# Key weights in two loads, a different head of the program and a new written order, in a fused attention and gated-mixer block

## The chip, the cores and the metric

The kernel runs on one core of one Trainium2 chip. The metric is the device time of one execution in microseconds, from launch to end; the time of before is the median of three runs. Beside it there is one profiled execution, whose instruction span is a little shorter than its own time.

## The reference

For 2048 tokens of width 512 (16 tiles of 128 tokens), all in bf16:

```
h  = x + A(layernorm(x))          # linear attention, 32 heads of 16
h2 = h + B(layernorm(h))          # gated mixer, inner width 896
A:  q, k, v = x @ wqkv
    pq, pk = phi(q), phi(k)       # phi(t) = t + 1 if t > 0 else exp(t), plus 1e-6
    kv = sum_s pk * v ; z = sum_s pk
    out = (pq @ kv) / (pq @ z) @ wo
B:  z1, z2 = gelu(x @ w_in), halves of 896
    g = w_sp @ layernorm(z2) + b_sp        # w_sp is 2048 x 2048, over tokens
    out = (z1 * g) @ w_out
```

## The kernel before

The program is recorded first as a list of 804 operations, each with its engine and with what it reads and writes. Two lists written into the file decide the rest: `ORDER` gives the order in which the operations are put on their engines (each of the five engines then runs its own part of it strictly in that order, waiting on semaphores for what it reads), and `SLOT` gives each temporary tile its place in a pool, among others the bank of the accumulator memory. The costs and due times that stand beside the operations in the code no longer decide anything.

The input x is loaded by SP in eight transfers (tiles 0, 1, 2-3, and after the key weights 4-5, 6-7, 8-9, 10-11 and 12-15), all issued by line L492. The key weights, columns 512 to 1024 of wqkv, come as one load of 512 KB, called wk, after tiles 2-3; the query weights, wq, come last.

The head then works tile by tile. VectorE computes mean and variance (statistics L568, their combination L572). 1/sigma is made in one of two ways: for tiles 0 to 3, one at a time, by ScalarE as a logarithm and an exponential (L582, L584); for tiles 4 to 15, in pairs, by GpSimd as an addition and a power (L587, L589). VectorE normalises (L603). Tiles 0 to 5 are transposed by TensorE (L633, four products of 128 columns) and copied out by ScalarE (L640). Tiles 6 to 15 are transposed by DMA, issued by SP (L625). With the transposed tile as weights, four products of 512 columns over the four blocks of the contraction make a tile's keys (L715). Pairs of tiles share a two-bank accumulator and go through phi: an exponential (L692) and in half the cases a relu (L694) on ScalarE, then VectorE (L695, and L698 or L701). The products L747 accumulate normalised x against phi of the keys, and L729 makes the queries.

TensorE begins with idle products of a constant (L556), so that it runs while x is on its way: a chain of 8 of 512 columns (`WARM`), then 4 more of 512, and 4 of 256 columns between the first transposes, 16 in all.

After the sums over all tiles (sum of keys L759, its transpose L772, the value product L796, the product with wo L814), four groups of 512 tokens each get their denominators (L829), their logarithm and exponential on ScalarE (L834, L836), a spreading product (L844), the output projection (L879) and the second layernorm. Value weights wv, output weights wo and w_in are issued on GpSimd's queue behind the last DMA transpose, in the order wv, w_in, wo. Then come the products with w_in (L911 and L942), the token mixer (L981, 448 products of 512 columns) and the last projection (L999) with its addition on VectorE (L1005) and the stores from SP (L1007). The last token tile is projected and stored in two halves of 256 columns.

Of the kernel before, what the change touches and what calls it, by code (L numbers as in the profile page):

```python
# [5 lines left out]
FP32 = mybir.dt.float32  # L6
BF16 = mybir.dt.bfloat16
ACT = mybir.ActivationFunctionType
ALU = mybir.AluOpType

P = 128
# [1 line left out]


ORDER = [
# [36 lines left out]
]  # L52
SLOT = [
# [6 lines left out]
]  # L60


# [292 lines left out]
def bass_sequential_preLN__linear_attn_block__mixer_gmlp__prompt_kernel(  # L355
# [25 lines left out]
    K_RELU = (1, 3, 5, 7)  # L381
    CENTRED = ()
    A_STATS = ()
    R_POOL = (4, 6, 8, 10, 12, 14)
    COPY_DVE = ()
    LN1 = [[0], [1], [2], [3], [4, 5], [6, 7], [8, 9], [10, 11], [12, 13], [14, 15]]
    N2_ACT = range(16)
    VIA_ACT = ((0, 0), (1, 0), (2, 0), (3, 0))
# [83 lines left out]
    def bank(i):  # L472
        return lambda a: a[:, i, :]
# [17 lines left out]
    def load(eng, name, dst, src, nbytes, bias=0.0, behind=(), cost=0.5):  # L491
        o = op(eng, cost, lambda e: e.dma_start(dst.ap(), src), w=[dst], dma=(name, False), nbytes=nbytes,  # L492
               bias=bias, land=2.3)
        for p in behind:
            o.deps[p] = True
        return o
# [10 lines left out]
    load_x("sp", 0, 1)  # L507
    load_x("sp", 1, 2)
    load_x("sp", 2, 4)
    load("sp", "wk", wqkv[:, D:2 * D], w3[:, :, D:2 * D], D * D * 2 + 50000)  # L510
    for a in (4, 6):
        load_x("sp", a, a + 2)
    for a in (8, 10):
# [95 lines left out]
    def normalise_act(dst, src, rs, nm, n=512):  # L609
        op("act", act_c(n, 2) + 0.04, lambda e: e.activation(dst.ap(), src.ap(), ACT.Identity, bias=nm.ap(), scale=rs.ap()),  # L610
           r=[src, rs, nm], w=[dst])

    def minus(m, rs, nm):
        op("pool", 0.25, lambda e: e.tensor_scalar(nm.ap(), m.ap(), -1.0, None, op0=ALU.mult), r=[m], w=[nm])
        op("pool", 0.25, lambda e: e.tensor_tensor(nm.ap(), nm.ap(), rs.ap(), ALU.mult), r=[nm, rs], w=[nm])
# [31 lines left out]
    for grp in LN1:  # L647
# [21 lines left out]
        rs_op[grp[0]] = g.ops[-1]  # L669
        for i, n in enumerate(grp):  # L670
            d = xn1[n, :]
            normalise(d, x[n, :], Row(st_x, n), 6, rs[i:i + 1], negative=n in A_STATS)
            transposed(n, lambda d=d: d, xT, n in X_BY_PE)

    for gate, n, cost, count in ((first[0], 512, 2 * MM, 3), (rs_op[0], 512, 2 * MM, 1), (tr_op[0], 256, MM, 2),
                                 (tr_op[1], 256, MM / 2, 2)):
        for i in range(count):
            keep_busy(n, cost, [], [gate] if gate.eng != "pe" else [])
            if gate.eng == "pe":
                g.ops[-1].after.append(gate)  # L680
# [25 lines left out]
    def kv_proj(p, col):  # L706
        t = Tile(PS, 2)
        for ti in range(2):
            n = 2 * p + ti
            lhs = xcT[:, n * P:(n + 1) * P] if n in CENTRED else xT[n // TPG][:, (n % TPG) * P:(n % TPG + 1) * P]  # L710
            rhs = wqkv[:, col:col + D]

            def mm(e, ti=ti, lhs=lhs):
                for c in range(KD):
                    i = e.matmul(t(bank(ti)).ap(), lhsT=lhs.ap()[:, c, :], rhs=rhs.ap()[:, c, :], start=(c == 0),  # L715
                                 stop=(c == KD - 1))
                return i
            k_pe.append(op("pe", 4 * MM, mm, r=[lhs, rhs], w=[t()]))
        return t

    def q_proj(gq, f):
# [294 lines left out]
                for n in range((tg - 1) * TPG, tg * TPG):  # L1016
                    project(n, [(0, D)])
    for n in range((NG - 1) * TPG, NT):
        project(n, [(0, D)] if n < NT - 1 else [(0, D // 2), (D // 2, D)])


    g.schedule()
# [55 lines left out]
```

## Time and profile before

| | us |
|---|---|
| median of three runs (243.93 to 244.29) | 244.26 |
| the profiled execution's own time | 243.96 |
| its instruction span | 242.2 |
| TensorE busy in the span | 238.3 |
| VectorE, ScalarE, GpSimd busy | 135.2, 85.1, 34.1 |

The granted TensorE clock is listed as 1.000 over the span. The busy time of TensorE includes the idle products at the start. Matmuls overlap in the records, so how long a product holds the engine is read from the distance of the starts, not from the listed duration.

### The profile page before, as it was taken

Reading aid. Unit: us, or ns where it says so; the run is one execution under the profiler, and the core shown is the slowest. Engines: PE = TensorE matmul, PEld = TensorE weight load, DVE = VectorE, ACT = ScalarE, POOL = GpSimd, SP = SyncE. Lnnn points to the kernel's source line nnn. Section 1 sums busy time; section 2 is a strip of 40 time slices with the busy share of each in tenths; the row PEclk is TensorE's granted clock in tenths of the full one; section 3 lists DMA queues with packets and bytes.
Section 4 is the critical chain, followed back from the end, with each engine's and each line's share of the span. In section 5 each row is a group of like instructions: output and inputs, shape, how many; then the busy total and the mean of one; then the engine's idle time right before and its main releaser. Section 6 shows DMA issues by size and latency. Waiting matters only on the chain.

```text
span 242.2 us, 3026 instructions
## 1 busy us (share of the span) xinstructions
PE 238.3 (98%) x1175; PEld 108.8 (45%) x1175; DVE 135.2 (56%) x269; ACT 85.1 (35%) x107; POOL 34.1 (14%) x87
## 2 busy tenths in 40 slices
PE   8999999999999999999999999999999999999995
PEld 3544443433444444445444444444444444444443
DVE  4999654589999967656533223251332513322443
ACT  3875744898588598564500010000000000000000
POOL 5316021002316542122100000000000000000000
DMA  6920459954324231459344444446200100000022
GB/s 199 321 43 18 94 106 337 232 122 96 46 43 128 47 46 22 87 119 231 88 108 92 107 86 95 100 108 94 83 0 0 65 24 0 0 0 3 0 87 87
DMA packets 55598, 21.57 MB, mean 89 GB/s; under 512 B 49472, under 2 KB 54720, under 8 KB 55584
## 3 DMA queue, kind: packets, MB, share of 16 engines
q1 hardware_dynamic: 54640, 17.05, 32.7%
q0 software_dynamic: 944, 4.33, 5.5%
q8 instruction: 9, 0.15, 0.3%
q14 instruction: 5, 0.04, 0.1%
HBM read 7.47 MB, written 2.10 MB: 40 GB/s over the span
## 4 chain that ended last, share of the span: by engine, by line
PE 91%; DVE 4%; DMA 2%; ACT 2%; SPq 1%; issue 0%
PE ps L981 40%; PE ps L942 10%; PE ps L911 10%; PE ps L999 10%; PE ps L747 6%; PE ps L879 5%; PE ps L715 5%; PE ps L729 4%; DMA xh<-in_A_x_dram 2%; DVE small L568 1%; SPq L492 1%; DVE xT_pq_z L698 1%; DVE xh L884 0%; DVE xT_pq_z L859 0%; DVE e L695 0%; PE ps L844 0%
## 5 line engine op out<-in xcount | busy, mean ns | idle before, releaser
L981 PE MATMUL ps<-wsp,pk_xn_z 128*128 128x512 bf16 x336 | 73.8, 379 | 0.0
L988 DVE TENSOR_TENSOR e<-ps,e 128x512 bf16<-128x512 f32 x28 | 19.4, 691 | 66.0 <-PE ps L981 66.0
L981 PEld LDWEIGHTS ps<-wsp,pk_xn_z 128*128 128x128 bf16 x336 | 32.8, 98 | 39.5
L942 PE MATMUL ps<-hT,win 128*128 128x512 bf16 x112 | 26.6, 379 | 0.0
L911 PE MATMUL ps<-win,hT 128*128 128x512 bf16 (+1 forms) x128 | 26.0, 353 | 0.0
L999 PE MATMUL ps<-wout,xT_pq_z 128*128 128x512 bf16 (+1 forms) x119 | 24.7, 367 | 0.0
L981 PE MATMUL ps<-wqkv_wsp,pk_xn_z 128*128 128x512 bf16 x112 | 24.3, 379 | 0.0
L947 ACT ACTIVATE xT_pq_z<-ps 128x1024 bf16<-128x1024 f32 (+1 forms) x16 | 14.4, 913 | 23.9 <-PE ps L942 23.9
L568 DVE BATCH_NORM_STATS2 small<-xh 128x6 f32<-128x512 bf16 x32 | 20.7, 678 | 3.3 <-DMA xh<-in_A_x_dram 3.3
L920 DVE BATCH_NORM_STATS2 small<-pk_xn_z 128x6 f32<-128x512 bf16 (+1 forms) x32 | 18.3, 611 | 7.2 <-ACT pk_xn_z L916 7.1
L692 ACT ACTIVATE e<-ps 128x1024 bf16<-128x1024 f32 x16 | 16.5, 1029 | 9.7 <-PE ps L715 6.1
L911 PEld LDWEIGHTS ps<-win,hT 128*128 128x128 bf16 x128 | 12.5, 98 | 12.7 <-ACT e L854 0.3
L916 ACT ACTIVATE pk_xn_z<-ps 128x896 bf16<-128x896 f32 x16 | 14.5, 914 | 8.9 <-PE ps L911 8.8
L1005 DVE TENSOR_TENSOR e<-ps,xh 128x512 bf16<-128x512 f32 (+1 forms) x17 | 11.2, 660 | 11.3 <-PE ps L999 11.3
L999 PEld LDWEIGHTS ps<-wout,xT_pq_z 128*128 128x128 bf16 x119 | 11.6, 98 | 12.8
L981 PEld LDWEIGHTS ps<-wqkv_wsp,pk_xn_z 128*128 128x128 bf16 x112 | 11.0, 98 | 13.2
L942 PEld LDWEIGHTS ps<-hT,win 128*128 128x128 bf16 x112 | 10.9, 98 | 12.6 <-ACT pk_xn_z L916 0.4
L589 POOL TENSOR_TENSOR small<-small 128x2 f32<-128x2 f32 x22 | 16.0, 727 | 1.2
L587 POOL TENSOR_SCALAR small<-small 128x2 f32<-128x2 f32 x22 | 6.4, 297 | 67.6 <-DVE small L572 67.4
L747 PE MATMUL ps<-pk_xn_z 128*128 128x512 bf16 x64 | 15.6, 379 | 0.0
L729 PE MATMUL ps<-xT_pq_z,wqkv_wsp 128*128 128x512 bf16 x64 | 15.5, 380 | 0.0
L715 PE MATMUL ps<-wqkv_wsp,xT_pq_z 128*128 128x512 bf16 x64 | 15.3, 379 | 0.0
(72 smaller groups left out, 191.0 us busy)
## 6 DMA issues: line engine op xcount, KB each, us to landing
out_dram<-e SPq DMA_DIRECT2D x15, 128.0 KB, 1.7
win<-in_B_w_in_dram POOLq DMA_DIRECT2D x1, 1792.0 KB, 9.2
xh<-in_A_x_dram SPq DMA_DIRECT2D x5, 256.0 KB, 4.7
wqkv_wsp<-in_A_wqkv_dram SPq DMA_DIRECT2D x2, 512.0 KB, 5.7
wout<-in_B_w_out_dram POOLq DMA_DIRECT2D x1, 896.0 KB, 6.4
wsp<-in_B_w_sp_dram SPq DMA_TRANSPOSE x48, 2.9
xh<-in_A_x_dram SPq DMA_DIRECT2D x1, 512.0 KB, 6.2
wqkv_wsp<-in_A_wqkv_dram POOLq DMA_DIRECT2D x1, 512.0 KB, 4.8
```

Source lines behind the costliest of these rows:

```text
L568: op("dve", dve_c(512), lambda e: e.bn_stats(s6.ap(), src.ap()), r=[src], w=[s6])
L589: return op("pool", 0.7, lambda e: e.tensor_tensor(dst.ap(), dst.ap(), h.ap(), ALU.pow), r=[dst, h], w=[dst])
L692: op("act", act_c(n), lambda e: e.activation(lo.ap(), t(flat).ap(), ACT.Exp), r=[t()], w=[lo])
L715: i = e.matmul(t(bank(ti)).ap(), lhsT=lhs.ap()[:, c, :], rhs=rhs.ap()[:, c, :], start=(c == 0), stop=(c == KD - 1))
L729: r_ = e.matmul(t(bank(i)).ap(), lhsT=lhs.ap()[:, c, :], rhs=rhs.ap()[:, c, :], start=(c == 0), stop=(c == KD - 1))
L747: r = e.matmul(txk[h](bank(i)).ap(), lhsT=xx.ap()[:, c * P:(c + 1) * P], rhs=kk.ap(), start=(n == 0), stop=(n == NT - 1))
L911: k = e.matmul(t(bank(i)).ap()[:, 0:b - a], lhsT=l.ap()[:, c, :], rhs=win[c, a:b].ap(), start=(c == 0), stop=(c == KD - 1))
L920: op("dve", dve_c(b - a), lambda e, s6=s6, src=src: e.bn_stats(s6.ap(), src.ap()), r=[src], w=[s6])
L942: k = e.matmul(t(bank(i)).ap(), lhsT=l.ap()[:, c, :], rhs=r_.ap()[:, c, :], start=(c == 0), stop=(c == KD - 1))
L981: k = e.matmul(t(bank(0)).ap(), lhsT=l.ap()[:, s - a, :], rhs=r_.ap()[:, s - a, :], start=(s == 0), stop=(s == NT - 1))
L988: op("dve", dve_c(512), lambda e: e.tensor_tensor(gb().ap(), t(bank(0)).ap(), bsp().ap()[:, tg * GW:(tg + 1) * GW], ALU.add), r=[t(), bsp( ...
L999: k = e.matmul(t(bank(0)).ap()[:, 0:b - a], lhsT=l.ap()[:, fc, :], rhs=wout[fc, a:b].ap(), start=(fc == 0), stop=(fc == KF - 1))
```

## The change

There are five edits to the text of the program, and two new lists.

- The key weights are loaded in two transfers of 256 KB, wk0 with the first two contraction blocks and wk1 with the other two. SP issues one more DMA ahead of tiles 4 to 15.
- The key products of tiles 0 and 1 are two operations of two products each, so that the first two wait for wk0 alone.
- There are 3 gated idle products after the chain of 8 instead of 8: two of 512 columns and one of 256, 11 in all.
- `R_POOL` no longer has the pair of tiles 4 and 5: its 1/sigma is made by ScalarE.
- The last token tile is projected and stored as 384 and 128 columns.
- `ORDER` and `SLOT` are written anew for the 802 operations. Other options that the diff adds (`N1_POOL`, `N1_ACT`) are empty and make no instruction.

```diff
-    R_POOL = (4, 6, 8, 10, 12, 14)
+    R_POOL = (6, 8, 10, 12, 14)
+    K_SPLIT = (0, 1)
...
-    load("sp", "wk", wqkv[:, D:2 * D], w3[:, :, D:2 * D], D * D * 2 + 50000)
+    for i in range(2):
+        load("sp", f"wk{i}", wqkv[2 * i:2 * i + 2, D:2 * D], w3[:, 2 * i:2 * i + 2, D:2 * D], D * D + 25000)
...
-    for gate, n, cost, count in ((first[0], 512, 2 * MM, 3), (rs_op[0], 512, 2 * MM, 1), (tr_op[0], 256, MM, 2),
-                                 (tr_op[1], 256, MM / 2, 2)):
+    for gate, n, cost, count in ((first[0], 512, 2 * MM, 2), (tr_op[0], 256, MM, 1)):
...
-            rhs = wqkv[:, col:col + D]
-
-            def mm(e, ti=ti, lhs=lhs):
-                for c in range(KD):
-                    i = e.matmul(t(bank(ti)).ap(), lhsT=lhs.ap()[:, c, :], rhs=rhs.ap()[:, c, :], start=(c == 0),
-                                 stop=(c == KD - 1))
-                return i
-            k_pe.append(op("pe", 4 * MM, mm, r=[lhs, rhs], w=[t()]))
+
+            for c0, c1 in ((0, 2), (2, KD)) if n in K_SPLIT else ((0, KD),):
+                part_r = wqkv[c0:c1, col:col + D]
+
+                def mm(e, ti=ti, lhs=lhs, c0=c0, c1=c1, part_r=part_r):
+                    for c in range(c0, c1):
+                        i = e.matmul(t(bank(ti)).ap(), lhsT=lhs.ap()[:, c, :], rhs=part_r.ap()[:, c - c0, :],
+                                     start=(c == 0), stop=(c == KD - 1))
+                    return i
+                k_pe.append(op("pe", (c1 - c0) * MM, mm, r=[lhs, part_r], w=[t()]))
...
-        project(n, [(0, D)] if n < NT - 1 else [(0, D // 2), (D // 2, D)])
+        project(n, [(0, D)] if n < NT - 1 else [(0, D - P), (D - P, D)])
```

What the new lists do to the first instructions of each engine (numbers are tiles; tr is a transpose, K the key products, copy is L640):

```
TensorE before  12 idle, tr0, 2 idle, tr1, 2 idle, K0, tr2, K1, K2, tr3, tr4, tr5, K3, K4, queries ...
TensorE after   10 idle, tr0, 1 idle, tr1, tr2, K0, K1, tr3, K2, tr4, tr5, K3, K4, K5, ...
VectorE before  stat0 stat1 comb0 comb1 stat2 norm0 comb2 norm1 stat3 norm2 comb3 stat4 stat5 comb4 comb5
                norm3 stat6 stat7 norm4 norm5 ...
VectorE after   stat0 stat1 comb0 comb1 stat2 stat3 comb2 norm0 comb3 norm1 norm2 stat4 stat5 comb4 comb5
                norm3 stat6 norm4 norm5 ...
ScalarE before  1/s of 0, 1, 2, copy0 copy1, 1/s of 3, copy2, exp of keys 0-1, copy3 copy4 copy5 ...
ScalarE after   1/s of 0, 1, 2, ln of 3, copy0, exp of 3, copy1 copy2, 1/s of 4-5, exp of keys 0-1, copy3 copy4 copy5 ...
```

GpSimd's three weight loads come in the order w_in, wv, wo. The rest of the list reorders the same operations.

More of the change, by code (lines that the diff above doesn't have):

```diff
@@ L383, in bass_sequential_preLN__linear_attn_block__mixer_gmlp__prompt_kernel @@
     A_STATS = ()
-    R_POOL = (4, 6, 8, 10, 12, 14)
+    R_POOL = (6, 8, 10, 12, 14)
     COPY_DVE = ()
+    K_SPLIT = (0, 1)
+    N1_POOL = ()
+    N1_ACT = ()
     LN1 = [[0], [1], [2], [3], [4, 5], [6, 7], [8, 9], [10, 11], [12, 13], [14, 15]]
@@ L611, in normalise_act, with normalise_pool @@
            r=[src, rs, nm], w=[dst])
+    def normalise_pool(dst, src, m, rs):
+        op("pool", 0.9, lambda e: e.tensor_scalar(dst.ap(), src.ap(), m.ap(), rs.ap(), op0=ALU.subtract,
+                                                  op1=ALU.mult), r=[src, m, rs], w=[dst])
     def minus(m, rs, nm):
@@ L671, in bass_sequential_preLN__linear_attn_block__mixer_gmlp__prompt_kernel @@
             d = xn1[n, :]
-            normalise(d, x[n, :], Row(st_x, n), 6, rs[i:i + 1], negative=n in A_STATS)
+            if n in N1_POOL:
+                normalise_pool(d, x[n, :], st_x[n, 6:7], rs[i:i + 1])
+            elif n in N1_ACT:
+                nm = small([1], FP32)
+                minus(st_x[n, 6:7], rs[i:i + 1], nm.all())
+                normalise_act(d, x[n, :], rs[i:i + 1], nm.all())
+            else:
+                normalise(d, x[n, :], Row(st_x, n), 6, rs[i:i + 1], negative=n in A_STATS)
             transposed(n, lambda d=d: d, xT, n in X_BY_PE)
-    for gate, n, cost, count in ((first[0], 512, 2 * MM, 3), (rs_op[0], 512, 2 * MM, 1), (tr_op[0], 256, MM, 2),
-                                 (tr_op[1], 256, MM / 2, 2)):
+    for gate, n, cost, count in ((first[0], 512, 2 * MM, 2), (tr_op[0], 256, MM, 1)):
         for i in range(count):
```

84 rows, old and new, of tables (ORDER, SLOT) are left out of this document.

## The prediction

> **What bounds the kernel now.** I read the page first, busy times and chain of waits, then the timelines of the first 16 us engine by engine, then those of 50 to 60 us and of the end.
>
> ```profile
> PE 238.3 (98%) x1175; PEld 108.8 (45%) x1175; DVE 135.2 (56%) x269; ACT 85.1 (35%) x107; POOL 34.1 (14%) x87
> PE 91%; DVE 4%; DMA 2%; ACT 2%; SPq 1%; issue 0%
> ```
>
> TensorE (PE) carries 91% of the chain that ends last. The change removes none of its useful products, so only three things can move the end: what PE waits for before its products run without a break, breaks later, and what follows its last product. The timeline of PE (start, length, instruction) shows the first:
>
> ```profile
> 0.83 5.25 PE L556 MATMUL ps<-const-bfloat16-1.0 128*128 128x512 bf16 x12 [0.83 <-PEq L1063]
> 5.91 0.40 PE L633 MATMUL ps<-small,pk_xn_z 128*128 128x128 bf16 x4
> 7.00 1.04 PE L715 MATMUL ps<-wqkv_wsp,xT_pq_z 128*128 128x512 bf16 x4
> 7.87 0.39 PE L633 MATMUL ps<-small,pk_xn_z 128*128 128x128 bf16 x4
> 8.09 1.89 PE L715 MATMUL ps<-wqkv_wsp,xT_pq_z 128*128 128x512 bf16 x8
> 9.82 0.39 PE L633 MATMUL ps<-small,pk_xn_z 128*128 128x128 bf16 x4
> 10.59 0.72 PE L633 MATMUL ps<-small,pk_xn_z 128*128 128x128 bf16 x8 [0.38 <-DVE pk_xn_z L603]
> 11.14 1.89 PE L715 MATMUL ps<-wqkv_wsp,xT_pq_z 128*128 128x512 bf16 x8
> ```
>
> Lengths overlap, so I divide the distance of starts by the count. A product of 512 columns holds PE for (9.82 - 8.09)/8 = 0.216 us; a transpose of four takes 0.22. Tile 3's transpose ends at 9.82 + 0.22 = 10.04, tile 4's begins at 10.59: 0.54 us lost. Transposes 4 and 5 take 0.55 instead of 0.45: 0.10 more. From 11.14 nearly all starts follow at their pitch. The idle products at the start are slower: (5.91 - 0.83)/12 = 0.42 each, twice 0.216, though the view of stages lists the granted clock as 1.00. I come back to that.
>
> The other engines, same stretch:
>
> ```profile
> 4.65 0.69 DVE L568 BATCH_NORM_STATS2 small<-xh 128x6 f32<-128x512 bf16 x1 [0.17 <-DMA xh<-in_A_x_dram]
> 5.26 0.40 DVE L603 TENSOR_SCALAR pk_xn_z<-xh,small 128x512 bf16<-128x512 bf16 x1
> 8.94 1.28 DVE L568 BATCH_NORM_STATS2 small<-xh 128x6 f32<-128x512 bf16 x2
> 10.13 0.72 DVE L603 TENSOR_SCALAR pk_xn_z<-xh,small 128x512 bf16<-128x512 bf16 x2
> 4.83 0.33 ACT L584 ACTIVATE small<-small 128x1 f32<-128x1 f32 x2
> 6.34 1.08 ACT L640 ACTIVATE xT_pq_z<-ps 128x512 bf16<-128x512 bf16 x2
> 9.16 1.02 ACT L692 ACTIVATE e<-ps 128x1024 bf16<-128x1024 f32 x1 [0.27 <-PE ps L715]
> 9.19 0.71 POOL L589 TENSOR_TENSOR small<-small 128x2 f32<-128x2 f32 x1
> ```
>
> Tile 4 is normalised at 10.13 because VectorE first does the statistics of 6 and 7 (8.94) and because GpSimd's power ends at 9.90. Tile 0 is normalised at 5.26, right behind the statistics of tile 2.
>
> **Key weights in two loads, keys of tiles 0 and 1 in halves: 0.** The shortest of the two loads of wqkv on SP's queue took 4.3 us, so wk, issued at 2.17, landed at 6.45. The first key product started at 7.00, just behind ScalarE's copy of tile 0 (6.34 + 0.60 = 6.94): the weights had 0.5 us to spare, and halves free nothing. If that cover were gone, the price would be the rest of the landing. The extra issue delays SP's next ones by 0.5 (wk's own issue: 2.17 to the next at 2.68). But tiles 4-5, issued at 2.68, were in use only at 7.22; a late issue hides in these 4.5 us as long as the transfers keep the memory busy. Ends: 0 and 0.5 later; I take 0, since the same bytes come in the same order.
>
> **The new head, step by step.** VectorE now does the statistics of 2 and 3 before it normalises tile 0: 4.65 + 1.29 less the overlap of 0.09 is 5.85; one combination (0.09 to the next start) gives 5.94 for the normalise and 6.34 for its end, against 5.66. Transposes of tile 0 start at 6.39, not 5.91. From there the old row gives copy and first key product 1.09 later (5.91 to 7.00): 7.48. Tile 1 is normalised at 6.34 and copied meanwhile. Keys of 0 and 1 take 8 x 0.216 = 1.73: 9.21. Tile 3's transpose 0.22, keys of tile 2 0.86, transposes of 4 and 5 0.45: 10.74.
>
> Are 4 and 5 there by then? Tiles 4-5 land as before (7.22); statistics and combinations to 8.64, tile 3's normalise to 8.94, one statistic (0.60) to 9.54. 1/sigma of 4 and 5 comes from ScalarE: combined at 8.72, then a logarithm (0.29) and an exponential (0.20) with their hand-overs, done by 9.3. So tile 4 is normalised at 9.55 to 9.95, 0.58 earlier, and its transposes, due at 10.29, no longer wait. The two ScalarE operations are ahead of the exponential of the first pair of keys, which PE releases only at 9.21 + 0.20 = 9.41 (8.96 to 9.16 in the old rows): they hide.
>
> What is late next is tile 3's copy, behind that exponential on ScalarE: 9.41 + 0.92 (its share when followed at once) = 10.33, + 0.60 = 10.93, hand-over 0.06: keys of tile 3 start at 10.99, 0.25 after PE is ready. In the old kernel they start at 11.14, and the same useful products lie before them in both. **Gain 0.15** (ends: 0.40 if the copy is in time, -0.3 if tile 4 is late again by the 0.5 above).
>
> **Fewer idle products: 0 if the rate of PE is what it was, and a risk.** Ten idle products end at about 5.05; PE is then idle until 6.39, 1.3 us where it had none. The rows show 0.42 per product until 5.91, after 5.08 us of unbroken work, and full rate from there on. If the rise comes at 5.9 again, all that counts runs at 0.216 and the edit costs nothing. If it comes later, each 512-column product meanwhile costs 0.21 more: that is the first rival.
>
> **GpSimd's three loads in a new order: 0.** All wait for the last DMA transpose.
>
> ```profile
> 34.55 0.98 POOL L492 DMA_DIRECT2D wqkv_wsp<-in_A_wqkv_dram  x1 [10.41 <-DMA xT_pq_z<-pk_xn_z]
> 45.79 1.06 PE L796 MATMUL ps<-wsp,wqkv_wsp 128*128 128x128 bf16 x16
> ```
>
> wv landed 4.8 after its issue, 39.35; w_in 9.2 after its own at 35.55, 44.75. Behind w_in, wv would be about 5.4 later, at 44.8; L796 is due at 45.6, and w_in itself only at 66.4. Cover 0.8 us; each microsecond beyond it is lost whole.
>
> **The rest of the order.** Between 11 and 120 us the products are the same and PE still has queries, projections and w_in products between waits. One break in the old trace is beyond the 0.1 us that PE loses at each change between 32-row and full products:
>
> ```profile
> 56.22 0.63 ACT L836 ACTIVATE wsp<-wsp 128x512 bf16<-128x512 f32 x1
> 56.99 0.40 PE L844 MATMUL ps<-wsp,small 32*128 32x512 bf16 x4
> ```
>
> L844 should follow L729 (55.85 + 0.86) at 56.71; it starts 0.28 later, behind ScalarE. The new order puts as many products (8) before it but begins the denominators later among ScalarE's work; I take half of the excess 0.19 as **gained, 0.1** (ends 0.2 gained; 0.2 lost, should a wait on a relu there take its place).
>
> **The last tile as 384 and 128: loses 0.13.**
>
> ```profile
> 239.76 0.42 DVE L1005 TENSOR_TENSOR e<-ps,xh 128x256 bf16<-128x256 f32 x1 [0.34 <-PE ps L999]
> out_dram<-e SPq DMA_DIRECT2D x2, 64.0 KB, 1.5
> ```
>
> VectorE takes 0.42 for 256 columns and 0.69 for 512, so about 0.56 for 384 and 0.29 for 128. Before: PE delivers at 239.72, VectorE ends at 240.18, the store is issued at 240.21. After, on the same clock: the 384 part is delivered 7 x 0.056 = 0.39 earlier, 239.34; VectorE 239.39 to 239.95; SP issues that store at 239.98 and needs 0.33 plus 0.04 until its next, so the 128-column store, ready at 240.18, goes out at 240.35: 0.13 late. A smaller store may land sooner, so the ends are 0 and 0.2.
>
> **Sum.** -0.15 - 0.1 + 0.13 = -0.12. The profiled execution of 243.96 (span 242.2 and 1.76 around it) would give 243.84; it lies 0.30 under the median of the runs, so in those terms 244.26 - 0.12 = 244.14. That is within 0.2% (0.49 us), about what a measurement of this kernel can tell from no change: forecast **same, 0.52**.
>
> **Rivals.**
> *PE stays at half rate into the keys: slower, 0.27.* For: the rise followed 5.08 us of unbroken work, and the new kernel breaks it at 5.05. Against: in the 5.08 us before 5.91 PE still works 4.2. Decisive is whether key products start at 0.43 apart at 7.5. Upper price: another 5.08 us from 6.39, a rise at 11.47, (11.47 - 7.48)/2 = 2.0 lost less the 0.25 waited anyway, 1.75; lower price 0. I take a point between, 1.0: 245.1.
> The Trainium skill, "TensorE: Matmul & The Clock Gate", Part 1, says that PE runs at half clock until an activity window of some 3.4 us has been busy, and that the windows run freely, so the rise differs from run to run; the two rates of the trace agree. By that rule a window missed at 5.9 ends next at 9.3, an estimated (9.3 - 7.5)/2 = 0.9 lost, in some executions and not in others; a window ending by 5.05 would cost nothing.
>
> *Nothing is late in the head and after: faster, 0.16.* Copy of tile 3 in time (-0.40), 0.19 regained at 57, and a quick last store (0): -0.59, 243.7. For: each is an end of a term above. Against: the copy is behind a 0.92 us exponential that PE itself releases late.
>
> *wv lands too late behind w_in: slower, 0.05.* If the last DMA transpose comes 1.5 us later than at 34.5, the 0.8 of cover is gone and L796 waits 0.7: 244.8. Against: tiles 8 to 15 are not normalised later by any row I see.
>
> *The split does what it is not needed for:* that is part of the forecast, since the weights were not awaited.
>
> **Numbers.** Faster 0.16, same 0.52, slower 0.27 + 0.05 = 0.32. The forecast's own range is 243.7 to 244.6, by the ends of its terms and the 0.2 that runs differ. Two in three of the clock cases lie under 245.4, half of the fast ones over 243.6: range 243.6 to 245.4.
>
> **What would show it.** Right: transposes of tile 0 near 6.4, keys of tile 0 at 7.5 and 0.216 apart, no wait of PE on L603 near 10.3, a wait on the copy, keys of tile 3 at 11.0, last two stores 0.37 apart. Wrong: key products 0.43 apart, L796 waiting for a DMA, or PE breaks over 0.3 us after 11.

## The result, and the profile after

The changed kernel takes 247.23 us (median of 6 runs, 245.63 to 247.90), the kernel before 244.27 in the same session (243.93 to 244.32): a ratio of 1.0112, 95% interval 1.0094 to 1.0129. The forecast was 244.14 with a range of 243.6 to 245.4. The kernel is slower, and by 1.8 us more than the range allowed. The profiled execution took 247.08 us, its span is 245.4.

The page of the changed kernel, busy times and then the chain that ended last, by engine:

```profile
PE 237.6 (97%) x1170; PEld 107.7 (44%) x1170; DVE 134.9 (55%) x269; ACT 84.8 (35%) x109; POOL 31.9 (13%) x85
PE 77%; DVE 10%; DMA 6%; ACT 3%; SPq 1%; POOL 1%; issue 1%; DVEq 0%
```

TensorE (PE) is busy 0.7 us less than before (fewer idle products), and the span is 3.2 longer: it waits more. The share of PE on the chain fell from 91% to 77%, that of DMA rose from 2% to 6%. The view of stages shows where (start and end, length, then busy time and count of PE, PEld, DVE, ACT and POOL, granted clock, DMA share, GB/s). First the kernel before, which was not shown by stages, then the changed one:

```profile
5.00:11.20 6.20, 5.79 (x44) 3.05 (x43) 6.04 (x19) 4.52 (x12) 1.11 (x3) 1.00 1.09 358
11.20:40.00 28.80, 28.80 (x136) 12.93 (x134) 21.95 (x48) 19.33 (x21) 8.29 (x13) 1.00 0.41 97
40.00:90.00 50.00, 49.85 (x282) 22.15 (x280) 43.04 (x81) 38.62 (x50) 14.36 (x37) 1.00 0.53 111
90.00:243.00 153.00, 149.72 (x711) 69.22 (x708) 62.30 (x118) 20.79 (x24) 6.72 (x13) 1.00 0.30 67
```

```profile
5.00:11.20 6.20, 4.55 (x37) 2.52 (x37) 5.54 (x16) 4.30 (x13) 0.00 (x0) 1.00 1.05 347
11.20:40.00 28.80, 27.70 (x129) 12.16 (x128) 22.17 (x51) 18.03 (x20) 7.34 (x13) 1.00 0.49 115
40.00:90.00 50.00, 48.70 (x275) 21.31 (x274) 41.31 (x76) 38.33 (x48) 11.40 (x29) 1.00 0.48 99
90.00:243.00 153.00, 152.74 (x725) 70.46 (x723) 63.95 (x125) 22.13 (x27) 9.57 (x21) 1.00 0.31 66
```

In the head PE is idle for 1.65 of 6.20 us, but most of that is time that idle products filled before. From 11.2 to 40 it was busy in all of the 28.8 us before and is idle for 1.10 now; from 40 to 90 it is idle for 1.30 instead of 0.15. (In the last row the old kernel has less only because it is done at 239.7.) The loss is in the stretch that the prediction called "the rest of the order". PE's timeline has it in four places:

```profile
22.12 1.04 PE L731 MATMUL ps<-wqkv_wsp,xT_pq_z 128*128 128x512 bf16 x4 [0.35 <-DMA xT_pq_z<-pk_xn_z]
23.90 1.04 PE L731 MATMUL ps<-wqkv_wsp,xT_pq_z 128*128 128x512 bf16 x4 [0.74 <-DMA xT_pq_z<-pk_xn_z]
71.79 0.40 PE L860 MATMUL ps<-wsp,small 32*128 32x512 bf16 x4 [0.69 <-ACT pk_xn_z L932]
84.54 1.89 PE L927 MATMUL ps<-win,hT 128*128 128x512 bf16 x8 [0.59 <-DMA hT<-xn]
```

The bracket counts from the modelled end of the product before. By the distance of starts, less 0.216 for a product of 512 columns, PE loses 0.52 and 0.90, then 0.85 and 0.75.

**22.1 and 23.9: keys of tiles 6 and 7.** They wait for the DMA transposes of their tiles. VectorE, then SP's queue in the changed kernel, then SP's queue before:

```profile
16.04 1.28 DVE L572 BATCH_NORM_STATS2 small<-xh 128x6 f32<-128x512 bf16 x2
17.23 0.72 DVE L607 TENSOR_SCALAR pk_xn_z<-xh,small 128x512 bf16<-128x512 bf16 x2
17.98 1.29 SPq L633 DMA_TRANSPOSE xT_pq_z<-pk_xn_z  x1
```

```profile
14.38 2.60 SPq L625 DMA_TRANSPOSE xT_pq_z<-pk_xn_z  x2
```

The keys of these two tiles in the kernel before:

```profile
20.64 1.89 PE L715 MATMUL ps<-wqkv_wsp,xT_pq_z 128*128 128x512 bf16 x8
```

The new order lets VectorE normalise tiles 6 and 7 at 17.23 instead of 12.96 and 13.96, behind statistics of later tiles and work of phi. The first transpose leaves 3.6 later. In the old kernel the two landed at 16.88 and 18.26, 3.8 and 3.2 us before their keys (20.64 and 21.50). On top of that they took 4.10 and 4.54 us to land (22.08 and 23.85) where they had taken 2.5. Without breaks their keys were due at 21.60 and 22.46, so with the old 2.5 us both would still have been in time, by 1.1 and 0.6: the wait needs the later issue and the slower transfer together.

**71.8: a spreading product behind the first gelu.** `SLOT` gives L860 an accumulator bank that ScalarE's first gelu has yet to read, and that gelu first loads its table:

```profile
69.44 1.28 ACT L932 ACT_TABLE_LOAD   x1
70.73 1.73 ACT L932 ACTIVATE pk_xn_z<-ps 128x896 bf16<-128x896 f32 x2
```

**84.5: w_in products of tile 5.** Its DMA transpose was issued at 78.56 and landed at 84.41, 5.85 us later. GpSimd issued the load of b_sp half a microsecond behind it; before (last line), that load went out at 73.51, ahead of the transposes:

```profile
78.56 1.27 SPq L633 DMA_TRANSPOSE hT<-xn  x1
79.09 0.64 POOL L495 DMA_DIRECT2D e<-in_B_b_sp_dram  x1 [3.23 <-DVE xT_pq_z L872]
73.51 0.64 POOL L492 DMA_DIRECT2D e<-in_B_b_sp_dram  x1 [0.24 <-DVE small L572]
```

The head itself comes out a little behind the old one (keys of tile 3 at 11.23 instead of 11.14):

```profile
6.48 0.38 PE L641 MATMUL ps<-small,pk_xn_z 128*128 128x128 bf16 x4 [1.75 <-DVE small L576]
7.55 1.90 PE L731 MATMUL ps<-wqkv_wsp,xT_pq_z 128*128 128x512 bf16 x8
9.57 0.40 PE L641 MATMUL ps<-small,pk_xn_z 128*128 128x128 bf16 x4
11.23 1.04 PE L731 MATMUL ps<-wqkv_wsp,xT_pq_z 128*128 128x512 bf16 x4
7.71 1.29 DVE L572 BATCH_NORM_STATS2 small<-xh 128x6 f32<-128x512 bf16 x2 [0.67 <-DMA xh<-in_A_x_dram]
```

### The profile page after: what moved, and what is told of

It reads as the page before. It is cut to its first block, busy times and chain, and to the rows that moved or that the text cites. A ratio compares the mean times of both kernels' runs of the same rounds, so it can differ in the third digit from the quotient of the medians.

```text
span 245.4 us, 3018 instructions
## 1 busy us (share of the span) xinstructions
PE 237.6 (97%) x1170; PEld 107.7 (44%) x1170; DVE 134.9 (55%) x269; ACT 84.8 (35%) x109; POOL 31.9 (13%) x85
## 4 chain that ended last, share of the span: by engine, by line
PE 77%; DVE 10%; DMA 6%; ACT 3%; SPq 1%; POOL 1%; issue 1%; DVEq 0%
PE ps L997 39%; PE ps L1015 10%; PE ps L927 8%; PE ps L958 8%; PE ps L763 4%; PE ps L731 3%; DVE small L572 3%; PE ps L745 3%; DMA hT<-xn 2%; DMA xT_pq_z<-pk_xn_z 2%; DMA xh<-in_A_x_dram 2%; ACT xn L614 1%; DVE e L709 1%; DVE xT_pq_z L875 1%; DVE xh L900 1%; DVE pk_xn_z L715 1%
## 5 line engine op out<-in xcount | busy, mean ns | idle before, releaser
L927 PE MATMUL ps<-win,hT 128*128 128x512 bf16 (+1 forms) x128 | 26.0, 353 | 0.6 <-DMA hT<-xn 0.6
L958 PE MATMUL ps<-hT,win 128*128 128x512 bf16 x112 | 26.1, 379 | 0.0
L1015 PE MATMUL ps<-wout,xT_pq_z 128*128 128x512 bf16 (+2 forms) x119 | 24.7, 366 | 0.0
L927 PEld LDWEIGHTS ps<-win,hT 128*128 128x128 bf16 x128 | 12.3, 98 | 13.5 <-issue 1.5
L1021 DVE TENSOR_TENSOR e<-ps,xh 128x512 bf16<-128x512 f32 (+2 forms) x17 | 11.1, 660 | 11.4 <-PE ps L1015 11.4
L593 POOL TENSOR_TENSOR small<-small 128x2 f32<-128x2 f32 x21 | 15.3, 729 | 1.1
L895 PE MATMUL ps<-pk_xn_z,xT_pq_z 128*128 128x512 bf16 x64 | 14.8, 379 | 0.0
```

What stands on the lines that cost most here:

```text
L593: return op("pool", 0.7, lambda e: e.tensor_tensor(dst.ap(), dst.ap(), h.ap(), ALU.pow), r=[dst, h], w=[dst])
L927: k = e.matmul(t(bank(i)).ap()[:, 0:b - a], lhsT=l.ap()[:, c, :], rhs=win[c, a:b].ap(), start=(c == 0), stop=(c == KD - 1))
L958: k = e.matmul(t(bank(i)).ap(), lhsT=l.ap()[:, c, :], rhs=r_.ap()[:, c, :], start=(c == 0), stop=(c == KD - 1))
L1015: k = e.matmul(t(bank(0)).ap()[:, 0:b - a], lhsT=l.ap()[:, fc, :], rhs=wout[fc, a:b].ap(), start=(fc == 0), stop=(fc == KF - 1))
```

## The experiments

Twelve kernels ran, in three groups of four, each with a profile and beside the kernel before. Every profiled execution can be cut in three: the start of the first key product of tile 3 (called K3), the body from there to the end of PE's last product, and the tail to the end of the span; 1.7 us lie outside the span in all of them. The useful products in the body are the same in all kernels, so its length shows the breaks alone. Some records of products are missing, and one that is missing moves what is read beside it by 0.216: in e5, e6 and e8 it is the first of K3's group (11, 11 and 7 records where the groups have 12, 12 and 8), and K3 is put 0.216 ahead of the first one that is there.

| profiled execution | tiles 4-5 of x land | K3 | body | tail |
|---|---|---|---|---|
| before | 7.19 | 11.14 | 228.58 | 2.51 |
| changed | 7.69 | 11.23 | 231.51 | 2.62 |
| e1 tiles 6, 7 early | 7.53 | 11.08 | 229.69 | 2.63 |
| e2 bank | 7.39 | 11.07 | 230.00 | 2.64 |
| e3 b_sp | 7.88 | 12.38 | 230.02 | 2.62 |
| e4 all three | 7.68 | 13.05 | 228.61 | 2.64 |
| e5 changed, 16 idle | 8.06 | 11.62 | 230.70 | 2.63 |
| e6 e4 with 16 idle | 8.01 | 11.57 | 228.56 | 2.63 |
| e7 before, 11 idle | 7.53 | 11.48 | 228.58 | 2.50 |
| e8 before, tail 384/128 | 7.54 | 11.48 | 228.59 | 2.64 |
| e9 before, two loads | 8.16 | 12.12 | 228.57 | 2.49 |
| e10 before, 1/sigma of 4-5 | 7.15 | 10.80 | 228.59 | 2.50 |
| e11 e6, tail 256/256 | 7.39 | 11.34 | 229.48 | 2.50 |
| e12 e11, one load | 8.75 | 12.29 | 229.80 | 2.50 |

**e1: tiles 6 and 7 early.** Operations 80, 79 and 81 are the statistics of tile 7 and the combinations of 6 and 7, 82 and 83 GpSimd's power, 84 to 87 the two normalisations and DMA transposes, 100 a statistic of a later tile.

```diff
- ... 142, 135, 72, 75, 100, 73, 65, 76, 136, 74, 143, 108, 77, 137, 152, 144, ...
+ ... 142, 135, 72, 75, 80, 79, 81, 82, 83, 73, 65, 76, 136, 74, 143, 108, 77, 137, 84, 85, 86, 87, 100, 152, 144, ...
```

> The changed kernel with one thing put back in the written order: tile 7's statistics, both combinations and 1/sigma of tiles 6 and 7 stand right behind the normalise of tile 5, and tiles 6 and 7 are normalised right behind the first pair's phi (tile 10's statistics go behind them). Theory of three waits: the transposes of tiles 6 and 7 are issued near 14.5 instead of 18.0, land before 18.5, ahead of the instruction fetch near 19.2, the key products at 22 no longer wait, and 1.4 us of 3.0 come back: about 245.8 against 247.2. Rival (a later rise of TensorE's clock, or the last stores, made the loss): no change, 247.2 within 0.4.

Measured: 245.22 (12 runs), ratio 1.0046 (1.0030 to 1.0062), 2.0 under the changed kernel's median. The queue of SP:

```profile
13.80 2.60 SPq L631 DMA_TRANSPOSE xT_pq_z<-pk_xn_z  x2
```

The two land 2.5 us after their issue, and the breaks at 22 and 24 are gone. The body is 1.82 shorter: 1.42 for them, and 0.37 because the wait for the transpose of hT's tile 5 came out at 0.38 instead of 0.75. The break at L860 stays at 0.85.

**e2: the bank.** The spreading product and ScalarE's copy of it (operations 298 and 299) go behind the third tile of w_in products.

```diff
- ... 380, 298, 430, 438, 336, 352, 299, 337, 439, 353, ...
+ ... 380, 430, 438, 336, 352, 337, 439, 298, 299, 353, ...
```

> The changed kernel with one thing moved: the spreading product of the last group of 512 tokens, and ScalarE's copy of its result, stand behind the third w_in tile instead of in front of it. Theory of three waits: the break of 0.85 before that product at 71.8 goes (0.1 stays), since its accumulator banks are free by then: 0.7 less, about 246.5. Rival (clock): no change, 247.2 within 0.4. Second rival: the break only moves to the next product that needs a bank that ScalarE's first gelu frees: 247.2.

Measured: 245.77 (9 runs), ratio 1.0063 (1.0041 to 1.0084). PE's timeline around the product:

```profile
71.21 1.25 PE L925 MATMUL ps<-win,hT 128*128 128x512 bf16 x6
72.39 0.40 PE L858 MATMUL ps<-wsp,small 32*128 32x512 bf16 x4
```

L858 is L860 of the changed kernel; it now follows without a wait. The body is 1.51 shorter, twice the 0.7 expected of the bank: the transpose of tile 5 was issued at 77.64, b_sp only at 78.99, and that wait went with it.

**e3: the load of b_sp behind the transposes of hT.** One operation, 611, moves behind 594.

```diff
- ... 443, 367, 611, 358, ... 485, 594, 486, ...
+ ... 443, 367, 358, ... 485, 594, 611, 486, ...
```

> The changed kernel with the load of b_sp issued on GpSimd right ahead of the load of w_out (near 100) instead of near 79. Theory of three waits: tile 5's second transpose takes 2.5 us again instead of 5.9, the break of 0.75 at 84.5 goes: about 246.5. Rival: the transpose is slow by an instruction fetch near 80 alone, and the break stays: 247.2 within 0.4.

Measured: 246.76 (5 runs), ratio 1.0106 (1.0084 to 1.0128). The transpose of tile 5 landed at 81.51, 2.55 after its issue, and PE did not wait for it:

```profile
84.20 1.89 PE L925 MATMUL ps<-win,hT 128*128 128x512 bf16 x8
```

The body is 1.49 shorter: 0.75 from this and 0.72 from the keys of tiles 6 and 7, which nothing here was to help (breaks of 0.21 and 0.49; the first product of tile 7 has no record). The median fell by only 0.5, and K3 shows a reason: in the profiled execution it began at 12.38, because most of the keys of tiles 0 and 1 ran at half rate (8 of them in 2.94 us):

```profile
7.83 2.94 PE L729 MATMUL ps<-wqkv_wsp,xT_pq_z 128*128 128x512 bf16 x8
```

**e4: all three.** The edits of e1, e2 and e3 together.

> The changed kernel with the three moves of the runs before together. Theory of three waits: 1.4 + 0.7 + 0.7 come back and about 0.2 over the kernel before is left: 244.4, within 0.4, and the spread of the executions shrinks. Rival (clock or stores): stays above 246.

Measured: 245.25 (12 runs, 243.95 to 246.08), ratio 1.0033 (1.0014 to 1.0053). The body is 228.61, the old kernel's to 0.03: **the three places are the whole loss in the body.** The runs fall in two groups, five from 243.95 to 244.57 and seven from 245.19 to 246.08, and the profiled one (246.02) is of the second. In that one the keys are the reason. PE's timeline and the view of stages:

```profile
6.83 0.38 PE L639 MATMUL ps<-small,pk_xn_z 128*128 128x128 bf16 x4 [1.92 <-DVE small L574]
7.90 3.54 PE L729 MATMUL ps<-wqkv_wsp,xT_pq_z 128*128 128x512 bf16 x8
```

```profile
7.00:11.20 4.20, 4.15 (x21) 1.76 (x19) 3.89 (x11) 2.30 (x7) 0.00 (x0) 0.60 1.04 352
```

Eight products start 0.43 apart (0.216 at full rate), at a granted clock of 0.60 over the stretch. With K3 at 11.1 instead of 13.05 this execution would have taken 244.1, which is the first group. For the rest of the second group the cause is not shown. One more of it has a mean granted clock of 0.993 over the span, as the profiled one has (half rate for 3.41 us); five have 1.000, which leaves both answers open, since e3's profile has 1.000 too: there the rate came up late, and the records of the clock begin only with the rise. The kernel before has single executions above 245 as well (9 of 96). And the median is no lower than e1's, though the body is 1.08 shorter.

**e5 and e6: the 16 idle products of before, in the changed kernel and in e4.**

```diff
-    for gate, n, cost, count in ((first[0], 512, 2 * MM, 2), (tr_op[0], 256, MM, 1)):
+    for gate, n, cost, count in ((first[0], 512, 2 * MM, 3), (rs_op[0], 512, 2 * MM, 1), (tr_op[0], 256, MM, 2),
+                                 (tr_op[1], 256, MM / 2, 2)):
```

> The changed kernel with the idle products of the kernel before (12 of 512 columns, 4 of 256) and nothing else undone. Theory of the clock beside the waits: TensorE runs without a long break until 5.9, so hardly an execution has key products at half rate: the three waits stay, the half-rate cost of some executions goes, about 0.7 less on the median, 246.5, and the spread of the executions halves. Rival (waits alone make the loss): no change, 247.2 within 0.3.

> The three moves of before together, with the idle products of the kernel before. Theory of the clock beside the waits: the upper group of executions of the run with the three moves alone (245.2 to 246.1) vanishes and the lower one (243.9 to 244.6) is left: median 244.2, within 0.3 of the kernel before. Rival (the upper group has another cause): median stays near 245.2.

Measured: 246.33 (6 runs), ratio 1.0081 (1.0054 to 1.0107), and 244.55 (12 runs), ratio 1.0018 (1.0004 to 1.0032). Against the same kernels with fewer idle products the medians are 0.9 and 0.7 lower, across sessions; the intervals of the ratios overlap in both pairs, so neither difference is clear of noise. The spread of e5 did not halve, as expected (2.2 us against 2.3). In e6, ten of twelve runs lie between 244.18 and 244.96; the upper group of e4 is down to two. The body of e6 is 228.56, the old kernel's to 0.02. So of the 3.0 us between the medians the three moves brought back 2.0 (e4), and with the idle products 2.7 (e6).

**e7: the kernel before with the fewer idle products of the change.** The reverse of the diff above, in the old order.

> The kernel before with the changed kernel's 11 idle products and nothing else. Theory of the clock: TensorE now breaks from about 5.05 to 5.9, so in some executions the key products run at half rate for up to 3.4 us: median 244.3 to 245.0 with single executions above 245.2. Rival: the clock needs no more idle products than these, 244.2 within 0.2.

Measured: 244.29 (12 runs), ratio 1.0006 (0.9995 to 1.0018): no change that can be measured. In its profile PE is idle 0.57 us ahead of tile 0's transposes, where the changed kernel has 1.75.

**e8: the kernel before with its last tile as 384 and 128.**

> The kernel before with the last token tile as 384 and 128 columns and nothing else. Theory: the second store waits for the first one's issue, 0.13 later, 244.33. Rival: a smaller store lands as much sooner, 244.2 or a little less.

Measured: 244.36 (12 runs), ratio 1.0007 (0.9997 to 1.0018). The time alone does not tell it from nothing. The tails of the table do: 2.62 to 2.64 in the eight kernels with 384 and 128, 2.49 to 2.51 in the six with 256 and 256; the difference is 0.13.

**e9: the kernel before with the key weights in two loads and the keys of tiles 0 and 1 in halves.** The diff is that of the change, these parts alone.

> The kernel before with one part of the change alone: the key weights in two loads of two contraction rows each, and the key products of tiles 0 and 1 in two halves, one behind each load; all sequences else as before. Theory A (the split costs the loads behind it): in the changed kernel wk came in at 5.87 and 6.97 instead of 6.44 and tile 4 of x at 7.69 instead of 7.19; here tile 4 lands at about 7.7 as well, VectorE's chain behind it starts 0.5 later, the transposes of tiles 6 and 7 and K3 with it, and the time rises by 0.2 to 0.5, to 244.4 to 244.7. Theory B (the term of the prediction, 0): the chain of tiles 0 to 3 decides, x4 is in time anyway, 244.2. Theory C: the first key product starts earlier on the first half (x0's transposes let it) and the time falls to 244.0.

Measured: 244.67 (12 runs, 243.92 to 245.76), ratio 1.0006 (0.9987 to 1.0026): -0.3 to +0.6 us, which decides nothing. In the profile tiles 4-5 landed at 8.16, and VectorE and the transposes of tile 4 wait for them:

```profile
8.19 1.29 DVE L569 BATCH_NORM_STATS2 small<-xh 128x6 f32<-128x512 bf16 x2 [0.98 <-DMA xh<-in_A_x_dram]
11.56 0.72 PE L634 MATMUL ps<-small,pk_xn_z 128*128 128x128 bf16 x8 [1.11 <-DVE pk_xn_z L604]
```

But here the second half of the weights was in at 6.28, earlier than the whole in the old profile (6.44). Tiles 4-5 landed 1.88 us after it, against 0.75 before and 0.72 in the changed kernel. SP issued them 0.5 later for the split (3.20 instead of 2.68); how much of the 1.88 that explains, this run does not show.

**e10: the kernel before with 1/sigma of the pair 4-5 by ScalarE**, their normalisations ahead of the second of the statistics of 6 and 7 (77, 79), their transposes right behind tile 3's. (The expectation says that tile 5 had this before; both tiles of the pair were with GpSimd, and TensorE transposes both.)

```diff
-    R_POOL = (4, 6, 8, 10, 12, 14)
+    R_POOL = (6, 8, 10, 12, 14)
- ... 62, 69, 77, 144, 70, 137, 79, 63, 71, 64, 74, 72, 78, 80, 75, 138, ...
+ ... 62, 69, 70, 77, 71, 74, 144, 137, 79, 63, 72, 75, 64, 78, 80, 138, ...
```

> The kernel before with one idea of the change alone: 1/sigma of tile 4 by ScalarE instead of GpSimd (tile 5 has it there already in before), the norms of tiles 4 and 5 and their DMA transposes ahead of the last statistics of tiles 6 and 7; nothing else moved. Theory A (the head's term, priced at -0.15): K3's wait at 11.14 shrinks to ScalarE's copy of tile 3 at about 11.0, the key products of tiles 4 and 5 never wait, and the time falls by 0.1 to 0.2, to about 244.0. Theory B: the pass over tiles 4 and 5 is off the chain that releases K3; no change that can be measured, 244.1 to 244.3. Theory C: the later statistics of tiles 6 and 7 push their DMA transposes back far enough that their keys wait as they do in the changed kernel, 244.5 or more.

Measured: 244.02 (12 runs), ratio 0.9988 (0.9972 to 1.0004). PE's timeline:

```profile
9.72 0.95 PE L632 MATMUL ps<-small,pk_xn_z 128*128 128x128 bf16 x12
10.80 1.47 PE L714 MATMUL ps<-wqkv_wsp,xT_pq_z 128*128 128x512 bf16 x6
```

The transposes of tiles 3, 4 and 5 run in one piece, and K3 begins at 10.80 instead of 11.14. So this part of the new head does what the prediction said of it. The median is 0.2 lower, the interval still holds no change.

**e11 and e12: e6 with the last tile in 256 and 256, and the same with the key weights in one load as well.**

> The kernel of the sixth experiment (changed kernel with tiles 6 and 7 early, the bank, b_sp's load and 16 idle products) with the last tile's output in two halves of 256 columns as before instead of 384 and 128. Theory A (tail term +0.13 to +0.2): 0.13 to 0.2 less than the sixth experiment's 244.55, so 244.35 to 244.4. Theory B (the tail is worth nothing): 244.55 again.

> The same as the run before it with the key weights in one load as well and the key products of tiles 0 and 1 whole. What is left of the change is the rest of its sequences. Theory A (the split costs about 0.3 to 0.5): tile 4 of x lands near 7.2, the wait at the transpose of tile 3 and K3 shrinks, and the time is 243.9 to 244.1, at or under before's 244.2. Theory B (the split costs nothing): 244.35 to 244.4, as the run before it.

Measured: 244.81 (12 runs), ratio 1.0009 (0.9988 to 1.0029), and 244.33 (13 runs), ratio 1.0000 (0.9984 to 1.0017). Neither tells its theories apart. The tails are 2.50, as expected. In e12 one load did not bring tiles 4-5 at 7.2: the weights landed at 6.93, x at 8.75, and K3 began at 12.29. In both bodies something returned that e6 did not have, a wait for a transpose of hT (0.70 and 1.05 us of PE's time), and PE loses 0.19 more ahead of the last 256 columns. The line is the transpose's in e12:

```profile
71.61 1.67 PE L925 MATMUL ps<-win,hT 128*128 128x512 bf16 x8 [0.89 <-DMA hT<-xn]
```

No version was shown to beat the kernel before; e10 comes nearest.

## Why the prediction was wrong

**The step that failed is "the rest of the order", priced at -0.1 with ends of 0.2 to either side.** It measured +2.9 in the profiled pair (body 231.51 against 228.58), and of the sign that the prediction named against itself, breaks of PE over 0.3 us after 11, there were four. It argued that the products between 11 and 120 us are the same and that PE has other products between waits, and then priced the one break that the *old* trace shows. That break (56.99, 0.28) did go, as forecast, but the body gained nothing by it: without the three moves it is the old one's. And a break list of the old kernel names what is late there; it says nothing of what has slack there and is moved. Three such slacks were used up: the 3.8 and 3.2 us between the landing of the transposes of tiles 6 and 7 and their keys (1.42 us lost); the freedom of the bank of the last spreading product (0.75 more than the usual 0.10); the free stretch in which b_sp was loaded (0.75). The moves are readable from the change without a run: in VectorE's part of `ORDER` the first normalisation of the pair stands behind the statistics of five later tiles instead of one, and of the moved DMAs the prediction followed only wv, w_in and wo. Their price is not: without the slower transfer tiles 6 and 7 would have kept 0.6 us of cover. The experiments show the cause, not only the place: with those moves undone (e4, e6) the body is the old one's.

**The head, -0.15: measured +0.09, in its mechanism right.** The row that fixes it is the landing of tiles 4-5. In the old order K3 began 3.94 to 3.96 us after it (before, e7, e8, e9), in the new order at full rate 3.54 to 3.95, median 3.56 (changed, e1, e2, e5, e6, e11, e12), in e10 3.65. So the new head is worth 0.3 to 0.4 for the same landing, at least twice my term. In the profiled pair x landed 0.50 later (7.69) and took it back: tile 3's normalise, queued on VectorE behind the statistics of tiles 4 and 5 at 7.71, released PE only at 9.57, where I had expected no wait. After that ScalarE's copy of tile 3 was last, ending near 11.19, as forecast; K3 followed at 11.23.

**The split of the load, 0 with an end of 0.5.** Tiles 4-5 land at 7.15 to 8.75 in the five profiles with one load (median 7.53) and at 7.39 to 8.16 in the nine with two (median 7.69). The difference, 0.16, is much smaller than the spread within each kind. That the split itself cost the 0.5 is not shown (e9, e12): loads differ by more than that from one execution to another of the same kind. I had taken 7.22 as a fixed time.

**Fewer idle products, 0 and the first rival: right as a risk.** Of the six profiles with 11 idle products, keys ran at half rate in two (e3, e4), in none of the eight with 16. In e3 and e4 K3 began 4.50 and 5.37 after the landing of x, so 0.9 to 1.8 later than the 3.56 above; I had named 1.0, bounds 0 and 1.75. The mean granted clock of the executions points the same way: it is 0.993 in 6 of the 44 of the new order with 11 idle products (changed, e1 to e4), and in none of the 43 with 16 (e5, e6, e11, e12). In the old order (e7) the same idle products cost nothing measurable; PE's gap before tile 0's transposes is 0.6 us there and 1.1 to 1.9 in the new one. In the changed kernel's own profile the rate was up by 7.55: its loss there has another cause.

The condition that I read off the old rows, a rise after 5.08 us of unbroken work, was an accident of that execution. The clock records show the first full rate at 3.86 to 6.73 us in eleven profiles and at 9.95 in e3 (the other two have no such records), though PE started its idle products at 0.83 in all of them.
In e4 the clock records of the trace show full rate for 3.41 us, half for 3.41, then full to the end of the products. The Trainium skill, "TensorE: Matmul & The Clock Gate", Part 1, says that the clock is granted by activity windows of about 3.4 us that run freely; the trace agrees. In e4 the 3.41 us at full rate held a break of 1.92 us, and the half rate followed; the changed kernel's break of 1.75 us came at full rate too and cost none. How long a break may be is not settled by two executions.

**The other terms.** The tail, +0.13: measured 0.13 in every profile (2.63 against 2.50). GpSimd's three loads, 0: w_in, wv and wo landed at 41.85, 43.41 and 45.19, and L812 (L796 of before) did not wait; the third rival did not occur. The second rival (243.7) needed K3 0.40 sooner, 0.19 less body and the old tail; no profile had the shorter body, and the earliest K3, 10.80 in e10, is 0.34 sooner.

## What to carry to other kernels

When a written order is replaced, list for each moved producer how long its result lay ready before its consumer in the old trace, and compare that with how far it moved; a list of the old waits cannot show it. Check every moved DMA, whatever its queue, for the transfers that it will meet, and every reused accumulator bank for who reads it last and what that reader must load first. Take the landing of a load as a range from several executions, and ask of a gap at the start whether it breaks the work that holds the clock up.

## What the runs showed of the hardware that I had not expected

The DMA records hold packets of a kind called instruction beside the data. In all fourteen traces nine of them have 16,384 bytes and last 0.9 to 1.6 us, at 19 to 21 us, 45 to 48 us, 61 to 73 us and later. The records do not name their engine. I take them for PE's, since the last ones (after 166 us) come where PE starts some 128 products from one to the next and ScalarE and GpSimd have nothing left to do. Most DMA transposes in flight at that time land late. In the changed kernel, with a fetch from 19.15 to 20.40, thirteen packets of the transposes that began between 19.84 and 20.14 took 1.07 to 1.36 us, where the median packet takes 0.018; the transposes of tiles 6 and 7 took 4.10 and 4.54 us there, and 2.5 in e1, where they had landed before the fetch. The page gives the fetches only as a sum:

```profile
q8 instruction: 9, 0.15, 0.3%
```

Of 309 transposes of x and hT between 12 and 95 us in the fourteen traces, 241 were in flight beside neither such a fetch nor the load of b_sp: 236 of them landed within 2.65 us of their issue, the longest took 3.01. Of the 43 beside a fetch alone, 28 took over 3.2, up to 4.54. The waits at L927 (in e12, L925) in e11 and e12 are of this kind (fetches at 67.27 and 69.10); in e6 the fetch fell at 69.84, when the last of its group was about to land (70.05), and there was no wait. That the fetch decides it is read from the records; no run moved it by itself.

The load of b_sp (512 KB, on GpSimd's queue) was in flight beside a transpose issued 0.5 us ahead of it in three kernels, and that one took 5.85 us, 5.48 in e1 and 4.67 in e5. Issued 1.3 us behind one (e2), it did not delay that one (2.55), and with the load moved to 103 us (e3) the same transpose took 2.55.
